# Attention with the scores made a second time, keys as rows, in place of transposed probabilities

## The chip, the cores and the metric

The kernel runs on one core of a Trainium2 chip. The metric is the device time of one execution in microseconds. A core has a matrix engine (TensorE, PE in the profile, with its weight loads as PEld), VectorE (DVE), ScalarE (ACT), GpSimd (POOL) and a queue engine, SyncE (SP), which here issues most DMAs. Each engine takes its instructions in a fixed order and waits at an instruction until what it needs is there.

## The reference, cut to what matters

The input x is 2048 rows of 1024 numbers. A layer norm is followed by an attention with a compressive memory, an output projection and a residual; then a second layer norm, a two-layer perceptron with GELU and another residual. The attention works on 32 heads of 32 columns and on four segments of 512 rows, in order:

```python
for s in range(N):                       # N = 4 segments, L = 512 rows
    qs, ks, vs = q[:, :, s], k[:, :, s], v[:, :, s]
    logits = einsum("bhqd,bhkd->bhqk", qs, ks) * scale + mask      # causal inside the segment
    a_dot = einsum("bhqk,bhkd->bhqd", softmax(logits), vs)
    a_mem = einsum("bhld,bhde->bhle", phi(qs), M) / (einsum("bhld,bhd->bhl", phi(qs), z) + 1e-6)
    o = g * a_mem + (1.0 - g) * a_dot                              # g = sigmoid(beta), one a head
    M, z = M + phi(ks)^T @ vs, z + sum(phi(ks))
```

phi(t) is t + 1 for positive t and exp(t) otherwise.

## The kernel before

All matmuls run in a rounded 32-bit type. To keep the precision of plain 32 bits, an operand is split into a high part (a cast) and a low part (what the cast left over), and a product is made of three matmuls (`mm3`, L110: high x high, high x low, low x high). The split of one operand is a copy with a cast, mostly on ACT, and a subtraction on DVE or POOL.

**Stages.** The 2048 rows go in two halves. Each half runs the first layer norm, the attention stage (`attention`, L201), the output projection (`wo_seg`, L536), the second layer norm and the first layer of the perceptron; the second layer comes last. A half has two segments (`sl` 0 and 1; `s` counts all four) and eight groups `g` of four heads, 128 columns of q, k and v.

**A dense unit** (`dense`, L268) makes k, q and v of one group and one segment, turned, columns as rows: 3 x 8 x 3 matmuls with 512 moving columns (`project`, L221; tiles `kps`, `qps`, `vps`). In between it evacuates them, computes phi of k and q, and collects the small products with the memory M in a list (`smalls`, L253), of which one is issued at a time by `one_small` between other matmuls. What has to wait for v (its transpose `vn` and its split `vs`, the memory's output `om`, its transpose `pom`, and the update of M) is in `late`, L330, which the next unit runs a step at a time. `stack`, L238, puts for each of the four heads the high and low parts of 32 rows of k (and of q) below each other in one tile of 96 rows, with three DMAs on SP's queue. One matmul over 96 rows then makes all three products of a score at once.

**A head** runs in a slot of six steps, and three heads are in work at a time: the current one, the one before (`p1`) and the one before that (`p2`). `PLAN`, L30, says which operation of which head stands in which step:

```python
PLAN = ('q1 S2', 'q0 n0 a0', 'q2 t0 a1', 'q3 n2 s0 o', 't1', 's1 t2')
```

- `q` (`qk`, L388), four times: 128 queries as rows against the keys up to them; a DVE operation adds the mask and finds the row maximum, then ACT takes the exponential and its sum (`soft`, L402).
- `n` (`norm`, L407): the reciprocal of the sums on DVE; POOL multiplies the probabilities by it and by 1 - g.
- `t` (`ptr`, L415): ten transposes a head on TensorE put the keys on rows, in three groups (512, 384 + 128 and 256 columns) in two PSUM buffers `ppt`; ACT copies the high part `pth`.
- `s`, `S` (`sub`, L433): DVE makes the low part `ptl` from the PSUM buffer, which is then free.
- `a` (`av`, L437): the products with V; the stationary block is 64 columns, V's high and low part. One PSUM buffer `po`.
- `o` (`av_out`, L455): DVE adds the two halves of `po` into `ot`; after a group's fourth head POOL adds the memory's part and SP stores `ot`.

**What sets the order.** `interleave`, L156, runs the dense unit and the heads of the unit before alternately, a step of each. The heads of a half's last unit run beside the output projection of its first segment, at 1.3 steps for each of the first 14 steps of the projection and 0.7 after (`RA`, `RH`, `RS`, L29, and `last`, L513). A scheduler then places the instructions of this stage on each engine by the order written and by when it takes them to be ready. Weights come in by `load_block`, L193: a DMA, a cast (`hi_eng`) and a subtraction. `load_o`, L523, reads a group's stored output back and splits it for the output projection.

## Time and profile before

| | |
|---|---|
| median of 3 runs | 2401.67 us (2401.52 to 2401.91) |
| the profiled execution | 2394.96 us, span 2393.2 us, granted clock 0.993 |
| transposes of the probabilities, PE L428 | x1280, mean length 277 ns |
| first scores, PE L396 | x512, mean length 318 ns |
| weighing of the probabilities, POOL L412 | x512, 322.2 us busy |
| exponentials, ACT L405 | x512, 287.8 us busy |
| maxima, DVE L397 | x512, 243.4 us busy |
| low parts of the probabilities, DVE L435 | x384, 227.2 us busy |

Times in the profile are us unless marked ns. A row of a group gives line, engine, operation, tiles written and read, shapes and count; then busy time, mean length of one, and the idle time of the engine just before them with what ended it. In the rows of instructions by time, the first number is the start from the span's beginning, the second the length (of all, where xN stands). Matmuls overlap: the next starts before the one ahead has ended.

### The profile page before, as it was taken

What the parts mean: (1) busy time and instruction counts of PE and PEld (TensorE: products, weight loads), DVE (VectorE), ACT (ScalarE), POOL (GpSimd) and SP (SyncE); (2) the same over time, 40 slices, a digit from 0 to 9 for tenths busy, and PEclk for the clock granted to TensorE, in tenths of its full rate; (3) what the DMA queues carried; (4) which work ended last, traced back from release to release, by engine and by line L of the source; (5) the groups of instructions that cost most, each with busy time, mean ns of one, the idle gap of its engine ahead of it and who ended that gap; (6) DMA issues with size and microseconds to landing.
All of it is one profiled execution on the core that took longest, in us unless ns stands there. A gap on an engine that the chain in (4) does not pass through costs nothing.

```text
span 2393.2 us, 35708 instructions
## 1 busy us (share of the span) xinstructions
PE 2308.3 (96%) x11873; PEld 1906.4 (80%) x11873; DVE 1628.4 (68%) x3470; ACT 1212.0 (51%) x2557; POOL 1065.5 (45%) x1011
## 2 busy tenths in 40 slices
PE   6999999999999989999999999999998989999999
PEld 5888888877787878888888877777886878888887
DVE  6777777775475664777777776466565888667763
ACT  4677676775363333677777776254343223232321
POOL 3444444444164442455555544245443554245430
PEclk9999999999999999999999999999999999999999
DMA  5333333333466654433333334366566976476762
GB/s 170 91 89 88 82 84 85 89 105 120 145 207 201 186 151 131 122 85 85 85 86 84 88 95 126 128 211 195 157 187 212 328 258 213 153 251 227 250 222 96
DMA packets 348161, 356.95 MB, mean 149 GB/s; under 512 B 26286, under 2 KB 251594, under 8 KB 347978
## 3 DMA queue, kind: packets, MB, share of 16 engines
q1 hardware_dynamic: 284810, 317.98, 44.3%
q10 hardware_dynamic: 63168, 36.71, 5.2%
q8 instruction: 94, 1.54, 0.3%
q14 instruction: 89, 0.73, 0.1%
HBM read 227.11 MB, written 77.14 MB: 127 GB/s over the span
## 4 chain that ended last, share of the span: by engine, by line
PE 72%; DVE 9%; ACT 6%; DMA 6%; issue 3%; POOL 3%; SPq 1%; ACTq 0%; DVEq 0%; POOLq 0%
PE po L1031 21%; PE bps L656 7%; PE ppt L428 5%; PE dps L656 5%; PE po L448 5%; PE pqk L396 3%; PE kps L111 2%; PE kps L112 2%; PE kps L113 2%; PE vps L111 2%; PE vps L112 2%; PE vps L113 2%; PE pwo L113 2%; PE pwo L111 2%; PE pwo L112 2%
## 5 line engine op out<-in xcount | busy, mean ns | idle before, releaser
L412 POOL TENSOR_SCALAR pr<-pr,nm,gate 128x128 f32<-128x128 f32 (+3 forms) x512 | 322.2, 639 | 409.0 <-DVE nm L409 307.3
L405 ACT ACTIVATE pr<-pr,mx 128x256 f32<-128x256 f32 (+3 forms) x512 | 287.8, 562 | 175.8 <-DVE mx L397 171.3
L397 DVE CUSTOM_DVE_ANT_0 pr<-pqk,mask 128x256 f32<-128x256 f32 (+3 forms) x512 | 243.4, 483 | 38.4 <-PE pqk L396 35.3
L435 DVE TENSOR_TENSOR ptl<-ppt,pth 128x512 fp32r<-128x512 f32 (+1 forms) x384 | 227.2, 597 | 53.5 <-ACT pth L430 51.4
L428 PE MATMUL ppt<-ident,pr 128*128 128x128 f32 x1280 | 222.7, 277 | 1.9 <-DVE ptl L435 1.8
L430 ACT CAST pth<-ppt 128x512 fp32r<-128x512 f32 (+1 forms) x384 | 194.1, 518 | 51.5 <-PE ppt L428 46.5
L92 POOL TENSOR_TENSOR wl<-wr,wh 128x1024 fp32r<-128x1024 f32 x64 | 152.9, 2390 | 103.2 <-ACT wh L91 48.4
L428 PEld LDWEIGHTS ppt<-ident,pr 128*128 128x128 f32 x1280 | 164.0, 140 | 32.1 <-DVE ptl L435 3.6
L1041 DVE TENSOR_TENSOR c<-c,po 128x512 f32<-128x512 f32 x160 | 105.2, 682 | 116.2 <-PE po L1031 115.8
L396 PE MATMUL pqk<-ks,qs 96*128 96x256 f32 (+3 forms) x512 | 162.7, 318 | 1.3 <-DVE mx L397 1.3
L448 PE MATMUL po<-ptl,vs 128*64 128x512 f32 (+3 forms) x512 | 154.2, 311 | 5.8 <-DVE ptl L435 5.6
L448 PE MATMUL po<-pth,vs 128*64 128x512 f32 (+3 forms) x512 | 155.5, 326 | 1.3 <-ACT pth L430 1.1
L888 POOL TENSOR_TENSOR w2r<-w2r 128x512 f32<-128x512 f32 x56 | 90.2, 1622 | 83.9 <-DMA w2r<-in_B_w 70.9
L1031 PE MATMUL po<-w2h,zh 128*128 128x512 f32 x378 | 122.2, 393 | 3.8 <-DVE zh L960 3.3
L409 DVE RECIPROCAL nm<-mx 128x2 f32<-128x2 f32 x256 | 42.2, 165 | 112.6 <-ACT pr L405 112.2
L396 PEld LDWEIGHTS pqk<-ks,qs 96*128 96x128 f32 x512 | 96.0, 188 | 26.4 <-DVE mx L397 6.3
L1031 PE MATMUL po<-w2h,hl 128*128 128x512 f32 x322 | 104.1, 393 | 6.4 <-DVE c L1041 6.4
L111 PE MATMUL vps<-yh,wh 128*128 128x512 f32 x256 | 109.0, 426 | 0.2 <-ACT omt L378 0.2
L111 PE MATMUL kps<-yh,wh 128*128 128x512 f32 x256 | 108.3, 423 | 0.0
L111 PE MATMUL qps<-yh,wh 128*128 128x512 f32 x256 | 107.2, 419 | 0.0
L111 PE MATMUL pwo<-oh,wh 128*128 128x512 f32 x256 | 104.8, 411 | 0.6 <-ACT oh L91 0.6
L113 PE MATMUL pwo<-oh,wl 128*128 128x512 f32 x256 | 101.5, 397 | 0.0
(233 smaller groups left out, 6751.5 us busy)
## 6 DMA issues: line engine op xcount, KB each, us to landing
hr<-h_dram SPq DMA_DIRECT2D x112, 448.0 KB, 5.0
w2r<-in_B_w SPq DMA_DIRECT2D x126, 256.0 KB, 3.9
r<-in_B_w SPq DMA_DIRECT2D x56, 512.0 KB, 4.5
h_dram<-ht ACTq DMA_DIRECT2D x84, 256.0 KB, 3.7
ks<-kh SPq DMA_DIRECT2D x256, 64.0 KB, 2.0
qs<-qh SPq DMA_DIRECT2D x256, 64.0 KB, 2.0
wr<-in_A_wo SPq DMA_DIRECT2D x32, 512.0 KB, 4.4
wx<-in_B_w SPq DMA_DIRECT2D x56, 256.0 KB, 3.6
```

Of the source, the lines that this page charges most:

```text
L111: nc.tensor.matmul(ps, ah, bh, start=first, stop=False)
L113: nc.tensor.matmul(ps, al, bh, start=False, stop=last)
L396: nc.tensor.matmul(pqk[:, :n], u["qs"][j][:, i * P:(i + 1) * P], u["ks"][j][:, 0:n], start=True, stop=True)
L397: nc.vector.tensor_tensor_reduce(out=st["pr"][:, offs[i]:offs[i] + n], in0=pqk[:, :n], in1=mask[:, 512 - n:512], op0=ALU.add, op1=ALU.min, ...
L405: nc.scalar.activation(pi, pi, AF.Exp, bias=mx[:, i:i + 1], scale=-1.0, accum_out=mx[:, 4 + i:5 + i])
L412: nc.gpsimd.tensor_scalar(pi, pi, nm[:, 4 + k:5 + k], gate[:, 1, 4 * g + j:4 * g + j + 1], op0=ALU.mult, op1=ALU.mult)
L428: nc.tensor.transpose(ppt[:, o:o + P], pr[:, offs[i] + jk * P:offs[i] + (jk + 1) * P], ident)
L430: nc.scalar.copy(pth[:, base:base + w], ppt[:, :w])
L435: nc.vector.tensor_tensor(o, x0, x1, op=ALU.subtract)
L448: nc.tensor.matmul(po[:, P * jk:], v, st[part][:, koff[jk]:koff[jk] + w], start=(jk, part) == (0, "pth"), stop=(jk, part) == (2, "ptl"))
L656: nc.tensor.matmul(ps, x_[:, c, :], y_[:, c, :], start=first and c == 0 and n == 0, stop=last and c == 3 and n == 2, skip_group_check=True)
L1031: nc.tensor.matmul(ps, x_[:, k], y_[k], start=opens and k == 0 and i == 0, stop=closes and k == self.KP - 1 and i == 2, skip_group_check=True)
```

## The change

The probabilities are no longer transposed. After the maxima of a head's four blocks of queries are known, one transpose turns them into four rows of 128, which are split into high and low and put by two DMAs as rows 96 and 97 below the head's stack of q; the stacks of k have ones there. A matmul over 98 rows with k as the stationary operand then gives, with the keys as rows, the scores less the row maximum of each query, ready for the exponential: `scores` in place of `ptr`. ACT takes the exponential inside the PSUM buffer and copies the high part; DVE makes the low part; POOL sets the masked half of the diagonal blocks to zero. The first scores now serve for the maxima alone, and their masked copy goes to a tile that nobody reads.

The sums of the probabilities come from 32 columns of ones between V's low and high parts (the stationary block has 96 columns). The output is weighed by (1 - g) / sum after the products: each head's row of sums is stored; after a group's fourth head they are loaded as 128x16, inverted and multiplied by 1 - g, stored, loaded spread over 32 rows a head, and multiplied into `ot` on POOL. A head is thereby in work for six slots instead of three (`pipe` of five). The gate of the memory's part moves into the copy of `pom`, and the output of a half's last group is split for the output projection directly, not stored and loaded.

Around it: the stacks of k and q are made in two parts, with six tiles each instead of five; phi is made of a ReLU, an exponential and one DVE operation that reads PSUM; some copies move between DVE, ACT and POOL, among them the high parts of the weights, from DVE to ACT; `RA` goes from 1.3 to 1.8 and `PLAN` is new. The diff, cut to its core:

```diff
-RA, RH, RS, PD, PS = 1.3, 14, 0.7, 28, 3
-PLAN = ('q1 S2', 'q0 n0 a0', 'q2 t0 a1', 'q3 n2 s0 o', 't1', 's1 t2')
+RA, RH, RS, PD, PS = 1.8, 14, 0.7, 28, 3
+PLAN = ('q3 O', 'q2 S2 a0', 'q1 q0 a1 L R Z', 't0', 'm t1 a2 s0', 't2 s1 F G')
...
+    for j in range(4):
+        nc.sync.dma_start(gate_t[32 * j:32 * j + 32, :],
+                          bass.AP(tensor=beta.tensor, offset=beta.offset + j, ap=[[0, 32], [4, NG]]))
...
+        ks_t = [ab.tile([98, 512], F32R, name=f"ks{i}") for i in range(6)]
+        for t in ks_t:
+            nc.vector.memset(raw(t[96:98, :]), 1.0)
+        vs_t = [ab.tile([P, 16, 96], F32R, name=f"vs{i}") for i in range(2)]
+        for t in vs_t:
+            nc.gpsimd.memset(raw(t[:, :, 32:64]), 1.0)
...
             nc.vector.tensor_tensor_reduce(
-                out=st["pr"][:, offs[i]:offs[i] + n], in0=pqk[:, :n], in1=mask[:, 512 - n:512],
-                op0=ALU.add, op1=ALU.min, scale=-SCALE, scalar=3.0e38, accum_out=st["mx"][:, i:i + 1])
-            soft(st, i)
+                out=junk[:, :n], in0=pqk[:, :n], in1=mask[:, 512 - n:512],
+                op0=ALU.add, op1=ALU.min, scale=-1.0, scalar=3.0e38, accum_out=st["mx"][:, i:i + 1])
...
+        def row(st):
+            qs = st["u"]["qs"][st["j"]]
+            pmx = ps_dense("pmx")[0:4, 0:P]
+            nc.tensor.transpose(pmx, st["mx"][:, 0:4], ident)
+            mr = ab.tile([4, 2, P], F32R, name="mr", bufs=2)
+            nc.scalar.copy(mr[:, 0, :], pmx)
+            nc.vector.tensor_tensor(mr[:, 1, :], pmx, raw(mr[:, 0, :]), op=ALU.subtract)
+            for n in range(2):
+                nc.sync.dma_start(raw(qs[96 + n:97 + n, :]).rearrange("o (i n) -> o i n", n=P),
+                                  raw(mr[:, n, :]))
...
             for jk in grp:
-                for i in range(jk, 4):
-                    one_small()
-                    o = koff[jk] - base + (i - jk) * P
-                    nc.tensor.transpose(ppt[:, o:o + P], pr[:, offs[i] + jk * P:offs[i] + (jk + 1) * P], ident)
-                    w += P
-            nc.scalar.copy(pth[:, base:base + w], ppt[:, :w])
+                k = 512 - P * jk
+                nc.tensor.matmul(ppt[:, w:w + k], u["ks"][j][:, jk * P:(jk + 1) * P], u["qs"][j][:, jk * P:512],
+                                 start=True, stop=True)
+                w += k
+            nc.scalar.activation(ppt[:, :w], ppt[:, :w], AF.Exp, scale=SCALE)
+            nc.scalar.copy(st["pp"][:, 0, base:base + w], ppt[:, :w])
...
+            nc.vector.tensor_tensor(pp[:, 1, base:base + w], e, raw(pp[:, 0, base:base + w]), op=ALU.subtract)
+            for o in (base, koff[3])[:1 + n % 2]:
+                d = pp[:, :, o:o + P]
+                nc.gpsimd.affine_select(d, d, pattern=[[0, 2], [1, P]], compare_op=ALU.is_ge, fill=0.0, base=0,
+                                        channel_multiplier=-1)
...
+            if n == 2:
+                c = st["c"] = ab.tile([64, 512], F32, name="c", bufs=1)
+                nc.scalar.copy(c, po[0:64, :])
+                lw = l_dram[u["s"]][u["g"]]
+                nc.sync.dma_start(lw[0, j:j + 1, :], c[32:33, :])
...
+        def fetched(st):        # step L
+                nc.sync.dma_start(u["li"], l_dram[u["s"]][u["g"]][0].rearrange("j (p n) -> (j p) n", n=16))
+        def weigh(st):          # step F
+                nc.vector.reciprocal(li, li)
+                nc.vector.tensor_scalar(li, li, rest_t[:, g:g + 1], None, op0=ALU.mult)
+                nc.sync.dma_start(l_dram[u["s"]][g][1].rearrange("j (p n) -> (j p) n", n=16), li)
+        def spread(st):         # step R
+                nc.sync.dma_start(u["lr"], l_dram[u["s"]][u["g"]][1].unsqueeze(1).to_broadcast([4, 32, 512]))
+        def close(st):          # step G
+                nc.gpsimd.tensor_tensor(ot, ot, u["lr"], op=ALU.mult)
+                if u["omt"] is not None:
+                    nc.gpsimd.tensor_tensor(ot, ot, u["omt"], op=ALU.add)
+                if g == NG - 1:
+                    oh, ol = acts["o", u["s"] % 2]
+                    split(None, ot, oh[:, g, :], ol[:, g, :], hi_eng="scalar", lo_eng="vector")
...
-        if sl == 0:
-            load_o(half, sl, NG - 1, tp)
```

More of the change, by code (lines that the diff above doesn't have):

```diff
@@ L486, in tail @@
         def tail():
[L487 to L488 removed]
+            for _ in range(4):
+                yield from slot(None)
         def weights(g):
```

202 lines of the change are left out of this document (103 added, 99 removed).

## The prediction

> **What bounds the kernel now.** I read the page first, for the busy shares and the chain, then the busy time by stretches of 50 us, for the stage that the change touches, and then TensorE's instructions in order of time there.
>
> ```profile
> span 2393.2 us, 35708 instructions
> ...
> PE 2308.3 (96%) x11873; PEld 1906.4 (80%) x11873; DVE 1628.4 (68%) x3470; ACT 1212.0 (51%) x2557; POOL 1065.5 (45%) x1011
> ...
> PE 72%; DVE 9%; ACT 6%; DMA 6%; issue 3%; POOL 3%; SPq 1%; ACTq 0%; DVEq 0%; POOLq 0%
> ```
>
> ```profile
> 300.00:350.00 50.00, 48.87 (x302) 40.99 (x301) 37.45 (x118) 35.53 (x91) 25.26 (x30) 1.00 0.36 89
> ...
> 1200.00:1250.00 50.00, 49.60 (x304) 41.72 (x303) 38.61 (x116) 36.78 (x92) 27.92 (x33) 1.00 0.35 89
> ```
>
> The columns of the second fence are the stretch, its length, busy us of PE, PEld, DVE, ACT and POOL, the granted clock, the DMA share and GB/s. These are attention stretches, one of each half. PE is idle for 1.1 and 0.4 of 50 us, at the full clock; DVE is busy for 37 to 39, ACT for 36 to 37, POOL for 25 to 28. PE also has 72% of the chain that ended last. So **TensorE's own work sets the pace**, and work taken from the other four is worth nothing by itself. What a matmul costs is not its length in the trace (the lengths overlap) but the distance from its start to the next start:
>
> ```profile
> 300.11 0.60 PE L428 MATMUL ppt<-ident,pr 128*128 128x128 f32 x4
> 300.46 0.48 PE L111 MATMUL vps<-yh,wh 128*128 128x512 f32 x1
> 300.77 0.40 PE L112 MATMUL vps<-yl,wh 128*128 128x512 f32 x1
> 301.01 0.39 PE L113 MATMUL vps<-yh,wl 128*128 128x512 f32 x1
> ...
> 302.16 0.28 PE L396 MATMUL pqk<-ks,qs 96*128 96x256 f32 x1
> 302.28 0.40 PE L111 MATMUL kps<-yh,wh 128*128 128x512 f32 x1
> ...
> 302.98 0.22 PE L396 MATMUL pqk<-ks,qs 96*128 96x128 f32 x1
> 303.04 0.39 PE L448 MATMUL po<-pth,vs 128*64 128x512 f32 x1
> 303.27 0.39 PE L448 MATMUL po<-ptl,vs 128*64 128x512 f32 x1
> 303.50 0.34 PE L448 MATMUL po<-pth,vs 128*64 128x384 f32 x1
> 303.67 0.34 PE L448 MATMUL po<-ptl,vs 128*64 128x384 f32 x1
> ```
>
> A matmul with 512 moving columns takes 0.23 us (303.04 to 303.27), one with 384 takes 0.17, with 256 0.12, with 128 0.06. Four transposes take 300.11 to 300.46, 0.35, and the matmul behind them takes 0.31 where its neighbours take 0.23 to 0.24; the extra 0.08 is theirs. So a transpose costs 0.43 / 4 = 0.108 us, more than a matmul of the same 128 columns.
>
> **The change, part by part.** There are 128 heads (32 heads in four segments). The sum is made against the profiled execution, 2394.96 us (span 2393.2); the median of the runs shown, 2401.67, is 6.7 higher, and 6.7 is added at the end.
>
> *TensorE's work.* Gone: 10 transposes of the probabilities a head, 1280 x 0.108 = 138.2 us. New: the scores a second time with the keys as rows, four matmuls a head with 512, 384, 256 and 128 columns, 0.23 + 0.17 + 0.12 + 0.06 = 0.58 us, x128 = 74.2; and one transpose of the row maxima a head, 128 x 0.108 = 13.8. Projections, first scores and the products with V keep their moving columns; V's stationary block grows from 64 to 96 columns for the ones. Net: 138.2 - 74.2 - 13.8 = **50.2 us less**.
>
> Short matmuls may not keep their 0.06: the four transposes above show 128 columns at 0.108 when short ones follow each other, and the change puts one 128-column score matmul and one small transpose a head among short products with V. Bounds: nothing, and 2 x 0.05 x 128 = 13 us. I take **+4**, near nothing, since the 128-column row above kept 0.06 with a wide matmul behind it.
>
> [...]
>
> *The other engines.* They get no credit; the question is what their lines now make TensorE wait for.
>
> ```profile
> L412 POOL TENSOR_SCALAR pr<-pr,nm,gate 128x512 f32<-128x512 f32 x128 | 99.9, 781 | 0.0
> L412 POOL TENSOR_SCALAR pr<-pr,nm,gate 128x256 f32<-128x256 f32 x128 | 73.9, 577 | 0.0
> L206 POOL TENSOR_SCALAR_AFFINE_SELECT mask<-mask 128x128 f32<-128x128 f32 x2 | 0.6, 292 | 0.1
> ```
>
> ```profile
> L405 ACT ACTIVATE pr<-pr,mx 128x512 f32<-128x512 f32 x128 | 92.8, 725 | 45.6 <-DVE mx L397 44.6
> L430 ACT CAST pth<-ppt 128x512 fp32r<-128x512 f32 x256 | 149.5, 584 | 40.4 <-PE ppt L428 35.6
> L229 ACT ACTIVATE e<-qps 128x512 f32<-128x512 f32 x24 | 14.5, 604 | 0.0
> ```
>
> POOL loses the four weighings a head and gains four selections that zero the masked half of a diagonal block (128x256, high and low part in one); each costs between 0.29 (the 128x128 row) and 0.58 us (the 128x256 weighing). I take 0.45, since 256 columns stand between the rows. POOL gets no fuller, but it now stands behind VectorE's subtraction and ahead of the products with V. ACT's exponentials go from four pieces (sum 1280 columns) with a sum read back to three without; one of 512 from PSUM to PSUM costs between 0.58 (the copy out of PSUM) and 0.73 us. I take 0.60, the exponential out of PSUM, an operation of the same kind. ACT also takes over the high parts of the weights from DVE. In the stretches above each of the three still had a quarter of its time free or more.
>
> *The wait that is added.* Before, a group of transposes in a `ppt` buffer was copied by ACT and subtracted by DVE; now an exponential comes ahead of both. Two buffers serve three groups a head, so the third waits for the first's subtraction:
>
> ```profile
> 305.16 0.60 PE L428 MATMUL ppt<-ident,pr 128*128 128x128 f32 x4
> ...
> 305.85 0.59 ACT L430 CAST pth<-ppt 128x512 fp32r<-128x512 f32 x1
> ...
> 306.47 0.69 DVE L435 TENSOR_TENSOR ptl<-ppt,pth 128x512 fp32r<-128x512 f32 x1
> ...
> 307.64 0.27 PE L428 MATMUL ppt<-ident,pr 128*128 128x128 f32 x1
> ```
>
> The buffer was held from 305.16 to 307.16, 2.00 us, and the next use came at 307.64 at the earliest. Now one matmul of 0.39 takes the place of four transposes of 0.60, and 0.60 us of exponential with some 0.1 for its start are added: 2.00 - 0.21 + 0.70 = 2.5 us, if ACT and DVE are free. In the order in which the changed kernel's instructions stand on TensorE, the work between the start of a head's first and third group sums, for eight heads in a row, to 2.97, 2.51, 2.64, 2.88, 2.74, 2.80, 2.35 and 2.59 us: mean 2.69. So the slack falls to 0.2 us, and whatever ACT has in hand when the group is done (0.6 us an operation) is time that TensorE stands. In its place dense matmuls have been moved ahead in that order, so part of it is already filled. Bounds: nothing, and 0.6 a head or 77 us. I take 0.08 a head, **+10 us**, because the same kind of wait today is nearly nothing:
>
> ```profile
> L428 PE MATMUL ppt<-ident,pr 128*128 128x128 f32 x1280 | 222.7, 277 | 1.9 <-DVE ptl L435 1.8
> ...
> L448 PE MATMUL po<-ptl,vs 128*64 128x512 f32 (+3 forms) x512 | 154.2, 311 | 5.8 <-DVE ptl L435 5.6
> ```
>
> Behind the waiting group stand, on TensorE, all the projections, and so everything.
>
> *The row of maxima.* It goes from VectorE to a transpose, a copy on ACT, a subtraction on DVE and two DMAs into two rows of the query stack, on SP's queue, where the stacks are also made:
>
> ```profile
> 324.65 1.17 SPq L243 DMA_DIRECT2D qs<-qh  x2
> ...
> 331.57 0.59 SPq L243 DMA_DIRECT2D qs<-ql  x1
> 332.26 0.53 SPq L195 DMA_DIRECT2D wr<-in_A_wk  x1
> ```
>
> ```profile
> qs<-qh SPq DMA_DIRECT2D x256, 64.0 KB, 2.0
> ...
> o_dram<-ot SPq DMA_DIRECT2D x32, 256.0 KB, 2.2
> ```
>
> Twelve stack DMAs are issued from 324.65 to 332.26, 0.634 us each, and land after 2.0. A dense unit has 24 of them, 15.2 us; the change adds 8 row DMAs, 4 stores of sums, and a load, a store and a spread of the weights, 15 issues; at between 0.35 and 0.63 each, 5 to 10 us. The queue stays under the unit's roughly 30 us. The worst place is the last head of a unit: from the end of the query projection the queue holds 15 stack DMAs and 7 others ahead of or with its rows, 15 x 0.634 + 7 x 0.35 = 12.0, with 2.0 to land and some 1.3 for the copy and subtraction in front: 15.3 us. TensorE's own work in its order from there to the scores that need the row is 18 us. I take **+2 us** for all heads (0 to 54, below).
>
> *The ends.* In the output projection the last group's output now comes straight from the heads that run beside it, some four heads in its first 14 steps instead of three, and the step behind waits for it. I take 2 us a half, **+4** (0 to 12). Four gate loads stand ahead of the first rows of x instead of one: three more issues, at most 0.53 each by the last row above, **+1**.
>
> Sum: -50.2 + 4 + 10 + 2 + 4 + 1 = -29 us. 2395 - 29 = 2366 in the profiled execution, 2366 + 6.7 = **2373 us** as a median.
>
> **The rivals.**
> (a) *No new wait, TensorE's saving whole.* For it: PE's idle time in the stage is 1 to 2% and the order as built has dense matmuls moved into the gaps. 2401.7 - 50 = 2351, 2349 with nothing for the ends. Against it: the slack of 0.2 us.
> (b) *The two `ppt` buffers become the bound: slower.* If ACT does the second group's exponential before the first's copy (the order as built has such places), the hold is 2.5 + 0.6 = 3.1 us against 2.69. One more 0.6 us operation ahead of it, as the dense part gives ACT, makes 3.7; between them stands a wait of 0.4 to 1.0 us, 0.6 a head: 77 us. Then -50 + 77 + 4 + 2 + 4 + 1 = +38, **2440**. It turns to no gain from (50 - 11) / 128 = 0.30 us a head.
> (c) *The row comes late on SP's queue: no gain.* If the load and the spread of the weights, which wait for stores to land (2.2 us each by the row above), hold the queue, 15.3 becomes 19.7 against 18: 1.7 us a unit, about 31 units, 53 us, **2402 to 2410**. Against it: the other three heads of a unit have shorter queues ahead.
> (d) *It doesn't do what it says:* the second scores are no cheaper than the transposes. The rows exclude it for TensorE (0.58 + 0.11 against 1.08 us a head); it could only come by way of (b) or (c).
>
> **How the numbers follow.** Forecast 0.44, (a) 0.22, (b) 0.20, (c) 0.10, and 0.04 for a saving beyond (a), from waits of today that go. Faster by over 0.2%, which is 4.8 us and about what a measurement of this kernel can tell from no change: forecast, (a) and the rest, 0.70. (c) is split, 0.07 the same and 0.03 slower; with (b), slower is 0.23. The range reaches from below (a), 2343, to 2430, most of the way to (b): it leaves out the far part of (b) and the rest, under 2 in 10. The forecast's own range is 2355 to 2392.
>
> **What would show it.** Right: in the attention stretches more matmuls in 50 us, the new scores start 0.23, 0.17 and 0.06 us apart, PE's idle time stays under 3 of 50 us, and waits of the new scores for the subtraction sum to 10 to 20 us. Wrong: PE idle for 4 us or more of 50, with the releaser DVE on `ppt` (b), a DMA of the stack on the first group (c), or POOL ahead of the products with V, which I cost at nothing because POOL has over 20 of 50 us free; if that cover is gone, at 0.45 us a head it is 58 us.

## The result, and the profile after

| | before | after |
|---|---|---|
| median | 2401.64 us (2401.52 to 2401.91, 4 runs) | 2482.85 us (2478.53 to 2487.31, 4 runs) |
| profiled execution | 2394.96 us, span 2393.2, clock 0.993 | 2479.71 us, span 2478.0, clock 0.988 |

The changed kernel is **slower**: ratio 1.0338, 95% interval 1.0316 to 1.0361. The forecast was 2373 with a range to 2430.

The page of the changed kernel, its span, its busy shares and the shares of the chain that ended last:

```profile
span 2478.0 us, 35389 instructions
...
PE 2342.4 (95%) x11233; PEld 1891.6 (76%) x11233; DVE 1599.4 (65%) x3280; ACT 1132.1 (46%) x2111; POOL 1004.6 (41%) x1095
...
PE 61%; DVE 10%; DMA 9%; issue 6%; ACT 5%; POOL 5%; SPq 3%; ACTq 0%; POOLq 0%; DVEq 0%
```

Every other engine is less busy than before, and PE's share of the chain is down from 72% to 61%: the chain now runs through the others more often. The two attention stretches shown before, and a stretch of each output projection (columns as before the change):

```profile
300.00:350.00 50.00, 48.63 (x260) 39.13 (x259) 34.14 (x102) 29.61 (x65) 18.82 (x31) 1.00 0.37 96
1200.00:1250.00 50.00, 46.02 (x243) 36.20 (x242) 35.13 (x102) 30.28 (x64) 24.12 (x36) 1.00 0.35 93
550.00:600.00 50.00, 45.06 (x208) 34.27 (x207) 29.93 (x86) 27.74 (x58) 16.87 (x29) 0.86 0.28 87
1500.00:1550.00 50.00, 43.74 (x201) 33.24 (x201) 31.49 (x89) 27.73 (x58) 19.97 (x33) 0.90 0.29 82
```

The same two stretches, likewise of the output projections, before:

```profile
550.00:600.00 50.00, 48.33 (x248) 39.62 (x248) 26.22 (x69) 24.54 (x43) 20.91 (x16) 1.00 0.42 129
1500.00:1550.00 50.00, 47.28 (x230) 38.63 (x230) 23.28 (x52) 14.19 (x21) 10.12 (x11) 0.97 0.47 153
```

PE is now idle for 1.4 and 4.0 of 50 us in the attention (1.1 and 0.4 before) and for 4.9 and 6.3 in the output projections (1.7 and 2.7 before). There the granted clock is 0.86 and 0.90, from 1.00 and 0.97.

**Where the 84.8 us of span went.** For every matmul I took the distance from its start to the next start, and took off what the prediction charged it: 0.227, 0.174, 0.117 and 0.060 us for 512, 384, 256 and 128 columns, 0.108 for a transpose (132 columns as 128). What is left over is summed apart, below 95 ns ("small gaps") and above ("stalls"), for the attention units and the two output projections:

| us | before | after | difference |
|---|---|---|---|
| TensorE's own work | 1158.4 | 1108.0 | -50.4 |
| small gaps | 33.9 | 62.4 | +28.5 |
| stalls in the attention units | 40.3 in 106 | 107.8 in 342 | +67.5 |
| stalls in the output projections | 16.4 in 31 | 44.6 in 122 | +28.2 |
| start of the first projection | 22.1 | 29.4 | +7.3 |
| all other stages | 1122.1 | 1125.8 | +3.7 |

The row of TensorE's own work is the number of matmuls times the prediction's prices. It shows that the planned matmuls went and came, and not that the prices hold. These are borne out by the distances: in the median the new scores with 512, 384 and 128 columns are followed after 0.237, 0.178 and 0.060 us, and the transposes before after 0.108. Behind the 256 columns, the third group of a head, 0.222 us pass instead of 0.117; most of these are among the stalls.

The loss is 464 stalls in place of 137, of 0.33 us each, and many small gaps. Not every stall is a wait: where the granted clock stood at 0.50, the 512-column matmuls at 1448.72 and 1449.14 us in the changed kernel were followed after 0.42 and 0.43 us, which leaves 0.19 and 0.20 over. Of the 464, 113 lie where the granted clock was below full (18 of the 137 before), and the lower clock cost an estimated 20.5 us in these stages (3.6 before): stretches of 5 us, each times what its granted clock lacked of 1. By the tile that waits, the stalls of the units went from 5.8 (then the transposes into it) to 40.1 at the second scores (`ppt`), from nothing to 15.7 at the transposes of the maxima (`pmx`), and from 10.4 to 14.9 at the products with V (`po`). The waits of the changed kernel, engine and line, what ended the wait, us, times and the longest:

```profile
ACT mr L430 <- PE pmx L428: 135.0, 60, 4.9
...
POOL ot L510 <- DMA lr<-l_dram: 84.0, 24, 6.8
...
PEld ppt L446 <- DVE pp L456: 49.0, 98, 1.7
...
PEld po L472 <- POOL pp L459: 15.2, 44, 2.1
...
PE ppt L446 <- DVE pp L456: 12.9, 34, 1.3
...
PE ppt L446 <- DMA qs<-mr: 7.8, 11, 1.0
```

```profile
SPq L520 <- POOL ot L512: 80.5, 19, 5.1
```

Here are the forecast's rivals side by side: the score buffers held by VectorE (b), the row of maxima late (c), POOL ahead of the products with V. One place shows how they hang together (start, length, engine, line, operation; the bracket is the idle time before, and what ended it):

```profile
1264.41 0.58 SPq L504 DMA_DIRECT2D lr<-l_dram  x1
...
1266.45 0.25 ACT L430 CAST mr<-pmx 4x128 fp32r<-4x128 f32 x1 [2.07 <-PE pmx L428]
...
1266.74 0.28 DVE L431 TENSOR_TENSOR mr<-pmx,mr 4x128 fp32r<-4x128 f32 x1 [0.69 <-ACT mr L430]
1266.95 0.58 SPq L433 DMA_DIRECT2D qs<-mr  x1
...
1269.63 1.28 POOL L510 TENSOR_TENSOR ot<-ot,lr 128x512 f32<-128x512 f32 x1 [4.26 <-DMA lr<-l_dram]
...
1270.99 1.28 POOL L512 TENSOR_TENSOR ot<-ot,omt 128x512 f32<-128x512 f32 x1
...
1272.30 0.35 SPq L520 DMA_DIRECT2D o_dram<-ot  x1
...
1272.74 0.58 SPq L433 DMA_DIRECT2D qs<-mr  x1
```

The row's first part leaves at 1266.95, its second only at 1272.74: between them in SP's queue stands the store of `ot`, which waits for POOL, which waits for the spread weights, whose transfer SP had issued at 1264.41. ACT had stood 2.07 us for the transposition of the maxima. Four engines that each work in order wait for one another.

### The profile page after: what moved, and what is told of

It is laid out like the page before. It is cut to its first block, busy times and chain, and to the rows that moved or that the text cites. A ratio compares the mean times of both kernels' runs of the same rounds, so it can differ in the third digit from the quotient of the medians.

```text
span 2478.0 us, 35389 instructions
## 1 busy us (share of the span) xinstructions
PE 2342.4 (95%) x11233; PEld 1891.6 (76%) x11233; DVE 1599.4 (65%) x3280; ACT 1132.1 (46%) x2111; POOL 1004.6 (41%) x1095
## 4 chain that ended last, share of the span: by engine, by line
PE 61%; DVE 10%; DMA 9%; issue 6%; ACT 5%; POOL 5%; SPq 3%; ACTq 0%; POOLq 0%; DVEq 0%
PE po L1087 17%; PE bps L712 7%; PE dps L712 5%; PE po L472 4%; PE pqk L419 2%; PE ppt L446 2%; SPq L257 2%; PE kps L115 2%; PE kps L114 2%; PE kps L116 2%; PE pwo L114 2%; DVE pp L456 2%; PE pwo L116 2%; PE pwo L115 2%; PE vps L116 1%
## 5 line engine op out<-in xcount | busy, mean ns | idle before, releaser
L459 POOL TENSOR_SCALAR_AFFINE_SELECT pp<-pp 128x256 fp32r<-128x256 f32 x512 | 204.4, 412 | 421.3 <-DVE pp L456 349.9
L420 DVE CUSTOM_DVE_ANT_0 junk<-pqk,mask 128x512 f32<-128x512 f32 (+3 forms) x512 | 248.3, 485 | 127.5 <-PE pqk L419 109.1
L456 DVE TENSOR_TENSOR pp<-ppt,pp 128x512 fp32r<-128x512 f32 (+1 forms) x384 | 225.0, 597 | 93.1 <-ACT pp L450 90.2
L472 PE MATMUL po<-pp,vs 128*96 128x512 f32 (+3 forms) x1024 | 247.0, 332 | 8.1 <-DVE ot L484 4.9
L449 ACT ACTIVATE ppt<-ppt 128x512 f32<-128x512 f32 (+1 forms) x384 | 192.5, 513 | 50.8 <-PE ppt L446 48.7
L450 ACT CAST pp<-ppt 128x512 fp32r<-128x512 f32 (+1 forms) x384 | 192.0, 517 | 6.4 <-POOL MZ L387 0.4
L472 PEld LDWEIGHTS po<-pp,vs 128*96 128x96 f32 x1024 | 148.5, 165 | 42.3 <-POOL pp L459 15.2
L446 PE MATMUL ppt<-qs,ks 98*128 98x512 f32 (+3 forms) x512 | 145.8, 347 | 25.2 <-DVE pp L456 12.9
L419 PE MATMUL pqk<-ks,qs 96*128 96x512 f32 (+3 forms) x512 | 157.0, 329 | 5.0 <-DVE mx L420 4.8
L116 PE MATMUL vps<-yh,wl 128*128 128x512 f32 x256 | 103.2, 403 | 0.0
```

The source lines that it names most:

```text
L116: nc.tensor.matmul(ps, al, bh, start=False, stop=last)
L419: nc.tensor.matmul(pqk[:, :n], u["qs"][j][0:96, i * P:(i + 1) * P], u["ks"][j][0:96, 0:n], start=True, stop=True)
L420: nc.vector.tensor_tensor_reduce(out=junk[:, :n], in0=pqk[:, :n], in1=mask[:, 512 - n:512], op0=ALU.add, op1=ALU.min, scale=-1.0, scalar=3 ...
L446: nc.tensor.matmul(ppt[:, w:w + k], u["ks"][j][:, jk * P:(jk + 1) * P], u["qs"][j][:, jk * P:512], start=True, stop=True)
L449: nc.scalar.activation(ppt[:, :w], ppt[:, :w], AF.Exp, scale=SCALE)
L456: nc.vector.tensor_tensor(pp[:, 1, base:base + w], e, raw(pp[:, 0, base:base + w]), op=ALU.subtract)
```

## The experiments

All are edits of the changed kernel (2483) and were timed beside the kernel before. "Work", "small" and "stalls" are the sums of the table above, over attention units and output projections.

| | median us | ratio to before, 95% interval | work | small | stalls |
|---|---|---|---|---|---|
| changed kernel | 2482.85 | 1.0338, 1.0316 to 1.0361 | 1108 | 62 | 152 |
| e1 one pass less on ACT | 2473.71 | 1.0307, 1.0292 to 1.0323 | 1108 | 62 | 143 |
| e2 no row | 2437.33 | 1.0159, 1.0144 to 1.0174 | 1094 | 63 | 119 |
| e3 store later | 2470.07 | 1.0298, 1.0282 to 1.0313 | 1108 | 63 | 142 |
| e4 gates by one transfer | 2485.86 | 1.0356, 1.0334 to 1.0377 | 1108 | 66 | 157 |
| e5 row made, not transferred | 2450.13 | 1.0229, 1.0205 to 1.0253 | 1108 | 63 | 124 |
| e6 weighing later | 2469.65 | 1.0307, 1.0288 to 1.0325 | 1108 | 63 | 141 |
| e7 short matmuls among scores | 2471.46 | 1.0313, 1.0293 to 1.0334 | 1108 | 67 | 142 |
| e8 slower heads in the projection | 2475.73 | 1.0342, 1.0317 to 1.0367 | 1108 | 64 | 149 |
| e9 row and sums on ACT's queue | 2494.66 | 1.0397, 1.0363 to 1.0432 | 1108 | 65 | 160 |
| e10 products with V later | 2480.28 | 1.0339, 1.0303 to 1.0374 | 1108 | 63 | 151 |
| e11 e4, e6, e7, e9, e10 together | 2464.76 | 1.0267, 1.0236 to 1.0297 | 1108 | 73 | 130 |
| e12 row transferred, not read | 2462.40 | 1.0273, 1.0246 to 1.0300 | 1108 | 66 | 128 |
| e13 V times a constant | 2489.00 | 1.0380, 1.0353 to 1.0407 | 1108 | 63 | 163 |
| e14 e12 and e13 | 2464.99 | 1.0284, 1.0260 to 1.0309 | 1108 | 63 | 135 |
| e15 exponential into SBUF | 2516.23 | 1.0499, 1.0476 to 1.0523 | 1108 | 65 | 187 |
| e16 no elementwise probabilities | 2436.54 | 1.0163, 1.0122 to 1.0204 | 1108 | 62 | 110 |
| e17 no path of the maximum | 2375.94 | 0.9913, 0.9897 to 0.9929 | 1020 | 55 | 144 |
| e18 neither path | 2340.90 | 0.9771, 0.9749 to 0.9794 | 1020 | 53 | 115 |

The kernel before, timed beside each group of runs, had medians from 2395.35 to 2401.64 us, so a difference of some 10 us between two medians of this table is not sure, and the ratios are the better comparison. By them e1, e4, e6, e7, e8, e10 and e13 are not told from the changed kernel: their intervals overlap its own, 1.0316 to 1.0361. That of e9 lies just above it.

**One cause at a time (e1 to e4).** The first theories were the two score buffers and SP's queue.

```diff
# e1
-            nc.scalar.activation(ppt[:, :w], ppt[:, :w], AF.Exp, scale=SCALE)
-            nc.scalar.copy(st["pp"][:, 0, base:base + w], ppt[:, :w])
+            nc.scalar.activation(st["pp"][:, 0, base:base + w], ppt[:, :w], AF.Exp, scale=SCALE)
# e2, with scores over 96 rows
-PLAN = ('q3 O', 'q2 S2 a0', 'q1 q0 a1 L R Z', 't0', 'm t1 a2 s0', 't2 s1 F G')
+PLAN = ('q3 O', 'q2 S2 a0', 'q1 q0 a1 L R Z', 't0', 't1 a2 s0', 't2 s1 F G')
# e3
+PLAN = ('q3 O', 'q2 S2 a0', 'q1 q0 a1 L R', 't0', 'm t1 a2 s0', 't2 s1 F G Z')
# e4
-    for j in range(4):
-        nc.sync.dma_start(gate_t[32 * j:32 * j + 32, :],
-                          bass.AP(tensor=beta.tensor, offset=beta.offset + j, ap=[[0, 32], [4, NG]]))
+    nc.sync.dma_start(bb, bass.AP(tensor=beta.tensor, offset=beta.offset, ap=[[0, P], [1, H]]))
+    for j in range(4):
+        nc.vector.tensor_copy(gate_t[32 * j:32 * j + 32, :],
+                              bb[32 * j:32 * j + 32, :].rearrange("p (g j) -> p j g", j=4)[:, j, :])
```

e1: 

> The exponential goes straight into the high part, so ACT has one operation a score group instead of two, and the low part is the score plus that (a sum with no meaning, which leaves out the low part of the probabilities); everything else is as in the changed kernel (2482.9 us). Theory 'buffer' (the third group of a head waits until the first group's PSUM buffer is free, and that chain is too long): some 0.6 us less on each hold takes the third group's waits away, 27 us in the units and 0.1 us behind each of 116, 35 us or more: under 2450. Theory 'queue' (the row of maxima comes late because SP's queue is blocked): under 10 us, 2473 to 2483. Theory 'length' (every chain of a head is too long for the slots, and taking one wait away lets the next show): 10 to 20 us, 2463 to 2473.

e2: 

> The row of maxima is left out (its transpose, copy, subtraction and two DMAs), and the second scores are made of 96 rows, without the maximum; the first scores and their maxima stay. TensorE's own work falls by 14 us. Theory 'queue': with it go the waits of the first group (14 us), of the row's transpose (17 us) and what stands behind them: 45 us or more, under 2438. Theory 'buffer': the 14 us of work and little more: 2460 to 2470. Theory 'length': 20 to 40 us, 2443 to 2463.

e3: 

> Only the store of a finished group's output is moved, from the third step of its slot to the last one, so that on SP's queue it stands behind work that is ready instead of ahead of a row of maxima. Theory 'queue' (the store waits for POOL, POOL for the spread weights, and the row behind it for the store): the waits of the store, 108 us on SP's queue, fall below 30, and the time by 10 to 25 us: 2458 to 2473. Theories 'buffer' and 'length': within 5 us of 2483.

e4: 

> The gates are loaded in one DMA with rows of 32 contiguous numbers, as before the change, and put in place by four small copies on DVE, instead of four DMAs of single numbers. The first projection started at 29.4 us against 22.1 before the change; if the four DMAs are the cause, it starts at 22 to 23 and the time falls by 7 us, 2476, by every theory of the rest. If the memory of ones on DVE or something else was the cause, it stays within 2 us.

The buffers alone fall: with one pass less in the hold, 9 us came back by the medians, which the ratios do not tell from nothing. The stalls at `ppt` in the units went from 40.1 to 37.1 us, and those at `pmx` rose from 15.7 to 23.5. The row is the largest single part: 45 us, of which 14 are its work on TensorE (1108 to 1094). But the kernel without it is still 1.6% slower than before, with 64 us less work. Its waits show what is late next:

```profile
PEld ppt L446 <- DVE pp L456: 27.5, 44, 1.5
...
ACT c L476 <- DMA l_dram<-c: 14.7, 13, 2.0
PE po L472 <- DVE ot L484: 14.2, 20, 1.8
```

The products with V wait for their one buffer `po`, held because ACT's copy into `c` waits until the row of sums has left `c` on SP's queue. The store three steps later (e3) gave 13 us, and the stalls at `ppt` fell from 40.1 to 30.3. That is the expected range, but not quite by the expected way: the store's waits for POOL's two operations on `ot` were to fall from 108 us below 30, and came to 73.6. SP's waits at the store, 80.5 in the changed kernel, in e3 (first row) and in e6 below (second row):

```profile
SPq L520 <- POOL ot L512: 69.1, 20, 4.1
...
SPq L523 <- POOL ot L512: 30.7, 15, 3.5
```

e4 did at the start what it should: the four gate transfers had delayed the first rows (first fence, changed kernel; second fence, e4), and the first projection began at 23.1 in place of 29.4.

```profile
0.79 1.87 SPq L64 DMA_DIRECT2D gate_t<-in_A_beta  x4
...
3.23 8.02 SPq L189 DMA_DIRECT2D xt<-in_A_x  x4
...
13.80 0.28 PE L76 MATMUL pb<-ident,b1r 28*128 28x28 f32 x1 [13.80 <-DMA b1r<-in_B_b]
```

```profile
0.79 0.39 SPq L64 DMA_DIRECT2D bb<-in_A_beta  x1
...
1.73 1.77 SPq L191 DMA_DIRECT2D xt<-in_A_x  x4
...
4.16 0.27 PE L78 MATMUL pb<-ident,b1r 28*128 28x28 f32 x1 [4.16 <-DMA b1r<-in_B_b]
```

Yet the time did not fall: in its profile the units are 5.4, the output projections 2.9 and the other stages 4.6 us longer than without the edit. Why a start 6 us earlier is lost again is not settled; the other stages, which no edit touches, differ by up to 6 us among these kernels.

**Place and pace (e5 to e8).**

```diff
# e5, with scores over 96 rows
-            for n in range(2):
-                nc.sync.dma_start(raw(qs[96 + n:97 + n, :]).rearrange("o (i n) -> o i n", n=P),
-                                  raw(mr[:, n, :]))
# e6, the last group of a half as it was
-                   "R": (p4, spread), "G": (p4, close), "Z": (p5, store_o)}
+                   "R": (p4, spread), "G": (p5, close), "Z": (p6, store_o)}
# e7
             for jk in grp:
+                one_small()
# e8, and for the last group of a half spread and close right behind weigh
-RA, RH, RS, PD, PS = 1.8, 14, 0.7, 28, 3
+RA, RH, RS, PD, PS = 1.3, 14, 0.7, 28, 3
```

e5: 

> Leaves out the two transfers that put the row of maxima under the stacked queries, and the scores take 96 rows, so the maximum isn't subtracted; the transposition of the maxima, ScalarE's copy of it and VectorE's subtraction stay. If the row costs time because its transfers stand on SP's queue behind stores that wait (theory 'queue'), this kernel comes out near the one without any row, whose time was 2437, plus the 14 us of TensorE's work that stay: 2445 to 2458. If the row costs time because ScalarE and VectorE, which work in order, stand waiting for the transposition (theory 'in order'), nothing is gained by taking the transfers away: 2472 to 2486.

e6: 

> The weighing of a unit's output (GpSimd's product with the spread weights) comes one head later, and its store after it, except for the last group of a half; nothing is left out. GpSimd stood 84 us in 24 waits for the spread weights, with the masking of the next probabilities behind it. If that stand holds TensorE's products with V (theory 'GpSimd in order'), 2483 falls by 15 to 40 us, to 2443 to 2468. If GpSimd has the time to spare, as the prediction had it, the time stays within 8 us of 2483.

e7: 

> A short matmul of the memory branch is issued ahead of every score matmul again, as the kernel before did with its transposes; nothing is left out. In the changed kernel a short matmul right behind another one took 113 ns in place of some 60. If this pacing by the loads of the stationary operand is a real part (theory 'loads'), 444 short matmuls gain up to 50 ns each, about 10 to 20 us: 2463 to 2473. If TensorE only waits elsewhere for what it no longer loses here: 2478 to 2488.

e8: 

> Of the last group of each half the weights are loaded, spread and used in the step after the sums instead of a head later, and the output projection goes back to 1.3 steps of the attention for each of its first 14 products, from 1.8; nothing is left out. In the changed kernel the output projection stages were 25 us longer than before, with the granted clock at 0.50 for some 10 us in each. If the faster pace of the attention, which leaves TensorE too few products to fill with, is the reason (theory 'too little to fill with'), 10 to 25 us come back: 2458 to 2473. If the stages are long because of the chain of each head at any pace: 2478 to 2490.

e5 speaks for the queue: with transposition, copy and subtraction kept and only the transfers gone, 33 us came back. With them went the scores' wait for the row, which e12 takes apart from the transfers. e6 gave 13 by the medians, a little less than it was expected to give, and not where it was expected: the stalls at the products with V went from 14.9 to 16.9 us, and those at `ppt` from 40.1 to 30.4, as in e3. Its store comes a head later too, and waits for 30.7 us in place of 80.5. That POOL's stand holds the products with V is not shown. e7 came out in the range of "loads", but not by its mechanism: the small gaps rose from 62 to 67, and the stalls fell by 10. e8 says that the quicker pace of the heads is not by itself what lengthens the output projections: they stayed at 274.6 us against 273.8.

**Other queue, other step, all together (e9 to e11).**

```diff
# e9
-            nc.scalar.copy(mr[:, 0, :], pmx)
+            nc.vector.tensor_copy(mr[:, 0, :], pmx)
-                nc.sync.dma_start(raw(qs[96 + n:97 + n, :]).rearrange("o (i n) -> o i n", n=P),
+                nc.scalar.dma_start(raw(qs[96 + n:97 + n, :]).rearrange("o (i n) -> o i n", n=P),
-                nc.sync.dma_start(lw[0, j:j + 1, :], c[32:33, :])
+                nc.scalar.dma_start(lw[0, j:j + 1, :], c[32:33, :])
# e10
-PLAN = ('q3 O', 'q2 S2 a0', 'q1 q0 a1 L R Z', 't0', 'm t1 a2 s0', 't2 s1 F G')
+PLAN = ('q3 O', 'q2 S2', 'q1 q0 a0 L R Z', 't0 a1', 'm t1 s0', 't2 s1 a2 F G')
```

e9: 

> The two transfers of the row of maxima and the transfer of the row of sums go out from ScalarE's queue in place of SP's, and VectorE makes both parts of the row, so that ScalarE stands for nothing but the issues (some 0.6 us each, three a head); nothing is left out. Leaving these row transfers out gave 2450, from 2483. If what they cost is their place on SP's queue behind stores and loads that wait (theory 'queue'), they cost little on a queue that does not wait: 2450 to 2465. If it is the transfer's own latency between the maxima and the scores (theory 'latency'), or if ScalarE has no time for the issues, the time stays at 2478 or above.

e10: 

> All products with V come one step later in the written order (steps 3, 4 and 6 in place of 2, 3 and 5), so that the chain from scores through exponential, copy, subtraction and mask has some 2.8 us more before the product needs it; nothing is left out. TensorE lost 30 us at the products with V. If the length of that chain is what they wait for (theory 'chain'), 8 to 25 us come back: 2458 to 2475. If they wait for buffers and for engines held up elsewhere, the wait goes with them: 2478 to 2495.

e11: 

> All edits that leave nothing out, together: row and sums on ScalarE's queue with the row made by VectorE, the weighing a head later, V products a step later, short matmuls among the scores, the gates from one transfer. If the parts add up (queue -25, weighing -13, short matmuls -11, start -7, V products -10), 2483 comes to 2410 to 2425. If they are the same waits seen at different places, no more comes back than by the best of them and the next: 2440 to 2455.

e9 does not decide about "the queue": off SP's queue the same transfers cost 12 us more in all, but the stalls at `ppt` and `pmx` fell (40.1 to 25.2, 15.7 to 6.3), and those at the products with V rose from 14.9 to 47.5. Waits of the kernel with the row on ACT's queue:

```profile
ACT ppt L449 <- PE ppt L446: 171.5, 107, 5.3
...
PEld po L472 <- POOL pp L459: 52.0, 74, 2.9
...
PE po L472 <- POOL pp L459: 35.3, 24, 2.8
...
ACT ppt L449 <- DMA qs<-mr: 30.1, 28, 1.2
```

Three issues a head (0.58 us for each part of the row, 0.22 for the sums) now stand among ACT's exponentials, and the weight loads of the products with V wait 52 us for POOL's masks in place of 15. e10 gave such products a step more and gained nothing: the stalls there fell from 14.9 to 9.5, and those at the first scores (`pqk`) rose from 3.2 to 17.5. All edits together (e11) gave 18 us, not the sum.

**Cutting the waits themselves (e12 to e15).** In e12 to e14 the work stays and only a dependency of TensorE goes.

```diff
# e12
-                nc.tensor.matmul(ppt[:, w:w + k], u["ks"][j][:, jk * P:(jk + 1) * P], u["qs"][j][:, jk * P:512],
+                nc.tensor.matmul(ppt[:, w:w + k], u["ks"][j][0:96, jk * P:(jk + 1) * P], u["qs"][j][0:96, jk * P:512],
# e13, and out=pqk in place of junk in the maxima
-                    nc.tensor.matmul(po[:, P * jk:], v, st["pp"][:, part, koff[jk]:koff[jk] + w],
+                    nc.tensor.matmul(po[:, P * jk:], v, fixed[:, 0:w],
# e15, with copy and subtraction from ex, out=pqk as in e13, and seven tmpr buffers instead of eight
-            nc.scalar.activation(ppt[:, :w], ppt[:, :w], AF.Exp, scale=SCALE)
+            nc.scalar.activation(ex[:, :w], ppt[:, :w], AF.Exp, scale=SCALE)
```

e12: 

> The scores take 96 rows and so don't read the row of maxima, which leaves the subtraction of the maximum out; the row is made and transferred by the same queue as in the changed kernel, for nobody. If the cost of the row is that TensorE's scores wait for it (theory 'edge'), this comes out like the kernel without its transfers, 2450: 2444 to 2458. If it is the time that its 256 transfers take on SP's queue from the other transfers (theory 'occupation'), nothing comes back: 2472 to 2488.

e13: 

> The products with V read a constant tile in place of the probabilities, which leaves the probabilities out of the output; all work on every engine stays, and only TensorE's wait for exponential, copy, subtraction and mask is cut. If the end of that chain is what holds TensorE (theory 'chain'), 25 to 45 us come back: 2438 to 2458. If the waits that it shows only stand for others that come a little later, 2465 to 2483.

e14: 

> Both cuts together: 96-row scores that don't read the row, and products with V from a constant tile. If the added time is the two waits (row and chain) on top of TensorE's smaller work, the time falls to 2345 to 2385, below the kernel before. If a third thing holds TensorE (the two score buffers, the short matmuls' loads, the lower granted clock), it stays at 2400 or above.

e15: 

> The exponential goes into a tile of its own in SBUF, from which copy and subtraction are made, so that a score buffer is free after one ScalarE pass of 0.6 us in place of three passes (2.5 us); the scratch output of the row maximum goes into the scores' own buffer to make room; nothing is left out. If the two score buffers hold TensorE (theory 'buffer'), the 41 us at the first and third groups of scores come back in part: 2445 to 2468. If the scores wait for the row and for ScalarE instead: 2474 to 2488.

e12 lies between its two theories: 20 us for the dependency, and 13 more (e5) when the transfers go too, though those two intervals touch. Cutting the end of the chain (e13) gave nothing, and both cuts (e14) no more than e12 alone. But e13 to e16, the scores' maxima still in them, also write the scratch output of the maxima to PSUM in place of SBUF, and in these runs that was not free: each of the 512 reads of a maximum behind it, 128x1 on DVE, took 135 ns in e13 where it took 82 in the changed kernel, 68.9 us in place of 42.1 in all, and 141 in place of 83 by the medians of e15 and the changed kernel. In e13 these are 27 us more on VectorE. No run has this edit alone, so what e13, e14 and e16 would give back without it stays open, and e13 does not show that the end of the chain costs nothing. e15 does what it says at its place, where the stalls at `ppt` fall from 40.1 to 22.0 us in the units, but those at `pmx` rise from 15.7 to 39.4 and those at `po` from 14.9 to 34.9. Part of that can be the slower maxima, so what the buffers alone are worth stays open.

**Whole paths (e16 to e18).**

```diff
# e16, on top of e14
-            nc.scalar.activation(ppt[:, :w], ppt[:, :w], AF.Exp, scale=SCALE)
-            nc.scalar.copy(st["pp"][:, 0, base:base + w], ppt[:, :w])
-            nc.vector.tensor_tensor(pp[:, 1, base:base + w], e, raw(pp[:, 0, base:base + w]), op=ALU.subtract)
-                nc.gpsimd.affine_select(d, d, pattern=[[0, 2], [1, P]], compare_op=ALU.is_ge, fill=0.0, base=0,
-                                        channel_multiplier=-1)
# e17, with scores over 96 rows; e18 is e16 and e17 together
-PLAN = ('q3 O', 'q2 S2 a0', 'q1 q0 a1 L R Z', 't0', 'm t1 a2 s0', 't2 s1 F G')
+PLAN = ('O', 'S2 a0', 'a1 L R Z', 't0', 't1 a2 s0', 't2 s1 F G')
```

e16: 

> No exponential, no copy, subtraction or mask of the probabilities; the products with V read a constant tile, and the scores take 96 rows without the row. The first scores, their maxima, the making of the row and its transfers stay, and TensorE's matmuls are those of the changed kernel. Stalls of TensorE of over 95 ns came to 99 us in the attention units against 32 before the change. If the elementwise work on the probabilities as a whole (6 us a head on ScalarE, VectorE and GpSimd, whatever its order) makes them (theory 'elementwise load'), 55 to 85 us come back: 2398 to 2428. If they come from TensorE's own queue, from the transfers or from the path of the maximum, the time stays over 2445.

e17: 

> No first scores, no maxima, no row (the subtraction of the maximum is left out); exponential, copy, subtraction, mask and products with V stay as they are in the changed kernel. TensorE's work falls by 87 us against it (first scores 73, transposition of the maxima 14), so 2396 if the waits stay what they are. If the path of the maximum makes the waits (theory 'path of the maximum'), another 50 to 80 us go: 2316 to 2346. If the elementwise work on the probabilities makes them, 2380 to 2400.

e18: 

> Both left out: no first scores, maxima or row, and no elementwise work on the probabilities; projections, second scores, products with V from a constant tile, memory branch, sums, weighing and output projection stay. What is left of TensorE's loss has nothing to do with either path. If the two paths together make the stalls, the time is 2483 less 87 of work, 66 of stalls and some 10 of the granted clock: 2310 to 2330. If more than 20 us of the loss stay with the short matmuls, the sums and the weighing: 2335 to 2370.

e16 and e17 came between their theories; e17 gave the 88 us of its work and 19 more. e18 came inside the theory that leaves more than 20 us of the loss outside both paths (2335 to 2370). Without the elementwise work the stalls at `ppt` are gone (40.1 to 1.4 us in the units) and those at `pmx` grow (15.7 to 28.8): what is late next is the transposition of the maxima. Without either path the products with V wait for `po` (52 us in 46 stalls), held by the transfer of the sums. Waits of e18:

```profile
POOL ot L503 <- DMA lr<-l_dram: 358.8, 31, 26.4
...
ACT c L469 <- DMA l_dram<-c: 115.7, 26, 7.7
...
PEld po L465 <- DVE ot L477: 60.5, 44, 4.6
PE po L465 <- DVE ot L477: 46.5, 31, 4.4
```

So three paths came with the change that end at TensorE (row of maxima, probabilities, sums), each of them passing ACT, DVE or POOL and two of them SP's queue. The first two are shown by taking them out, the third only by its waits in e2 and e18. Taken out alone, the transfers of the row are worth 33 us, the probabilities (with both dependencies, and with the slower maxima) 46; the probabilities and the whole path of the maximum together, net of work, 54 (142 less 88). The stalls that remain in e18, 115 against 57 before, are for an estimated 34 us the lower granted clock, worked out as above (3.6 before), and were not taken apart further: a run without the sums was not tried. The edits around the change (the high parts of the weights on ACT, the new phi, the stacks in two parts) stand in every run, and none was taken back, so a part of what remains may be theirs. e17 is faster than both kernels, but it takes the exponential of unreduced scores, so it is no replacement.

## Why the prediction was wrong, by its own steps

**TensorE's work: right.** The planned matmuls went and came, -50.4 us at the prediction's prices where -50.2 was forecast, and the distances above bear the prices out, but for the short matmuls of the next term.

**Short matmuls, +4 (0 to 13): too small.** The small gaps grew by 28.5 us, short waits among them. Products with V and short matmuls in turn, changed kernel:

```profile
322.31 0.25 PE L472 MATMUL po<-pp,vs 128*96 128x128 f32 x1
322.39 0.27 PE L274 MATMUL pmm<-vs,pkh 128*128 128x128 f32 x1
322.50 0.25 PE L472 MATMUL po<-pp,vs 128*96 128x128 f32 x1
322.59 0.28 PE L274 MATMUL pmm<-vs,pkl 128*128 128x128 f32 x1
322.70 0.31 PE L472 MATMUL po<-pp,vs 128*96 128x256 f32 x1
```

They start 0.08 to 0.11 us apart, not 0.06. In these rows a block of 96 columns is followed after 0.08 to 0.09, one of 128 after 0.11. V's wider block was charged nothing; what it costs by itself is not shown, since no run changes the width alone.

**The wait that is added, +10 (0 to 77), and the row, +2 (0 to 54): these are the steps that failed.** The stalls at the second scores grew by 34 us in the units, 0.27 us a head, close to the 0.30 from which rival (b) was to turn the sign; transposes that wait for the maxima add 16; removing the row's transfers gives back 33. Mechanisms and places were named, and the bounds held each; what failed is that every wait was priced by its own edge, with the other engines taken as ready. e1, e9 and e10 show that it cannot be: where the stalls at one edge shrink, those at another grow. The ground for the low price, "each of the three still had a quarter of its time free", was nearly true (DVE was free for 11.4 of 50 us in the second stretch) and worth nothing: ACT, DVE and POOL are less busy after than before.

**POOL ahead of the products with V, nothing (58 if its cover goes):** too low, but small by itself. 15.2 us of waits of the weight loads end at POOL's masks, and the weighing a head later (e6) did not lower the stalls there. A mask took less than taken, 0.41 us:

```profile
L459 POOL TENSOR_SCALAR_AFFINE_SELECT pp<-pp 128x256 fp32r<-128x256 f32 x512 | 204.4, 412 | 421.3 <-DVE pp L456 349.9
```

**The ends, +4 (0 to 12):** the output projections grew by 25.5 us (248.3 to 273.8). The reason that I gave, the quicker heads, is not it (e8). About half is the granted clock, which the prediction did not have at all: summed over stretches of 5 us, the time lost below full clock in these two stages went from 1.8 to 15.4 us, an estimate in the same way as above.

**Gate loads, +1:** +7.3 at the first projection, by the delay of the transfers behind them; but taking it away (e4) did not shorten the kernel.

**Rivals.** (a) is excluded by the stalls and (d) by TensorE's work. (b), 2440, named the right wait and sign, not that it would be one of three. (c) named SP's queue: the weights do hold it, by way of the store that waits for them (80.5 us), but with the row off that queue (e9) the kernel was slower. One sign of being right, "more matmuls in 50 us", could not have come: a head has five short matmuls in place of ten transposes.

## What to carry to other kernels

DVE and ACT, busy for 34.1 and 35.1 and for 29.6 and 30.3 of 50 us in the two attention stretches, were here not free for a chain that TensorE waited on: price a new hand-over by how many engines that work in order it passes and what stands ahead on each, and price all new hand-overs together. Where cutting a wait gives back less than the wait, look where stalls have grown, take out whole paths, and compare the sums. Where a test edit brings a second edit with it, time that one alone as well; here this is missing for the scratch output of the maxima. Work taken from TensorE is a gain only as far as the paths that feed it are shorter than what is left: here 50.4 us less of it came with 84.8 us more of span.

## What the runs showed of the hardware

In three places of the changed kernel the granted clock fell to 0.50 though TensorE had been busy for a part of each of the three us before. The first of them, in the first output projection, in stretches of 1 us (PE's busy time is the first number behind the length, the clock the third from the end):

```profile
554.00:555.00 1.00, 1.00 (x9) 0.89 (x7) 0.67 (x5) 0.00 (x0) 0.41 (x1) 1.00 0.63 90
555.00:556.00 1.00, 0.57 (x4) 0.19 (x2) 0.57 (x1) 0.00 (x0) 0.00 (x0) 1.00 0.63 229
556.00:557.00 1.00, 0.49 (x2) 0.29 (x2) 0.71 (x5) 0.00 (x0) 0.00 (x0) 1.00 0.26 100
557.00:558.00 1.00, 0.75 (x3) 0.35 (x3) 0.71 (x4) 0.00 (x0) 0.00 (x0) 0.85 0.26 99
558.00:559.00 1.00, 1.00 (x5) 0.93 (x5) 0.00 (x0) 0.00 (x0) 0.00 (x0) 0.50 0.05 15
...
570.00:571.00 1.00, 1.00 (x7) 1.00 (x6) 1.00 (x3) 0.48 (x1) 0.41 (x1) 0.50 0.91 269
571.00:572.00 1.00, 1.00 (x6) 0.90 (x5) 0.46 (x3) 0.97 (x3) 0.00 (x0) 0.82 0.56 167
572.00:573.00 1.00, 1.00 (x8) 0.75 (x6) 0.97 (x2) 0.84 (x3) 0.48 (x2) 1.00 0.07 22
```

Three us at 57, 49 and 75% busy came before the fall, and the clock stayed at 0.50 for some 13 us, in the last ten of which TensorE was busy almost throughout. The falls at 1448.6 and 1513.4 us came likewise, behind three us of 57, 73 and 25% and of 42, 100 and 39%. That the row of stalls brought the fall is the author's reading; no run takes the two apart. What the lower clock did to the matmuls behind it is measured: a 512-column matmul was followed after 0.42 and 0.43 us (1448.72 and 1449.14 us), where the same two lines at 300.15 and 300.38 us, at the full clock, were followed after 0.23 and 0.24. If the reading holds, a stall of TensorE cost twice in these places.
